# Attention with a local window and a low-rank mixer MLP on one core: q and k turned by VectorE, off-diagonal keys in a tile of their own, a written order

## The chip, the cores and the metric

The kernel runs on one NeuronCore of a Trainium2 chip. The metric is the device time of one execution in microseconds (us). One execution was also profiled; times below that have two decimals come from it and count from the start of its span. Engines: TensorE (PE; PEld is its weight load), VectorE (DVE), ScalarE (ACT), GpSimd (POOL), SyncE (SP, whose instructions here are DMA issues only). DMAs are issued by POOL (queue q0) and by SP (queue q1) and carried by 16 DMA engines.

## The reference

Four batches, 8 heads, 768 tokens, head size 64. Attention keeps the first 8 keys and, for each query, the 96 last ones, with a bias that falls with distance; its output, rows of 512, goes through a mixer over tokens of rank 32 and a two-layer MLP of 2048.

```python
# q, k, v: (4, 8, 768, 64)   n_global = 8, n_local = 96
scores = scale * np.matmul(q, k.transpose(0, 1, 3, 2))
rel = pos[:, None] - pos[None, :]
is_global = pos[None, :] < n_global
is_local = (rel >= 0) & (rel < n_local)
dist = np.where(is_global & ~is_local, n_local, np.abs(rel))
scores = np.where(is_global | is_local, scores - slopes * dist, -1e9)
a = softmax(scores)
x = (a @ v) with the heads side by side                # (4, 768, 512)
h = x.transpose(0, 2, 1) @ U @ V                       # U: (768, 32), V: (32, 768)
u = x + h.transpose(0, 2, 1)
out = u + np.maximum(u @ w_ch1, 0.0) @ w_ch2           # 512 -> 2048 -> 512, float32
```

## The kernel before

All products are float16 with float32 sums. A *pair* is two heads of one batch; there are 16, p = 0 to 15, four for each batch. The work is cut into named tasks, each a handful of instructions on one engine. Names carry the pair, or the batch and a number:

- `lk`, `lq`, `lv` (`ld`, line 450, and `ldv`, line 460) load k, q, v of a pair on POOL's queue, cast from float32 to float16 on the way. Pair 0's k and q come by SP in float32 and are cast by `Ck0`, `Cq0`. Of the first seven pairs but that one, q comes with 6 tokens to a partition (one run of 1536 bytes for each partition and head) and k with three groups of 2 tokens (runs of 512 bytes). Pairs 7 to 15 come in runs of 256 bytes (one token of one head), 1,536 for each q, k or v, in two issues for q and k and in one for v.
- `TK`, `TQ` (line 600) turn k and q so that the head's columns are the partitions: 12 TensorE transposes each, for pairs 0 to 6, and `EK`, `EQ` copy the result out of PSUM. For pairs 7 to 15 `EK`, `EQ` are DMA transposes on SP (line 624).
- `KO` (line 643) puts the 32 first keys beside each block of keys. A block of queries meets its own block of keys (the diagonal) and one off-diagonal block: the last 96 keys of the block before, and the first 32. In this kernel those lie side by side because each block of `kT` is 160 wide. `VO` and `VG` (lines 650 to 660) build the rows of v that belong to it, which shifts them by 32 partitions: in pairs 0 and 1 by POOL copies, from pair 2 on by a DMA on SP.
- `SB` adds the bias of batch 0 into PSUM as a product of the identity with a table for each head (line 689); `S` are the scores (line 708), row-tiled, so that two heads of 64 rows share the array; `EX` the exp on ACT; `MK` multiplies by exp of the bias (masks) on DVE in batches 1 to 3.
- `PV` is the product with v (lines 804, 805), `RC` and `NM` divide by the sums, `XC` casts x to float16, `UP` (lines 778, 788) turns x by six products with the identity and forms x times U by six products with u as weights; `TE` copies the latter out, `HM` (line 911) adds the product with V, `E0` to `E1` copy u into `uT`. For pairs 12 to 15 x is turned by a DMA transpose on SP (`XD`, line 880) and added by DVE.
- `M1a`, `M1b` (line 967) are the first MLP product, 16 steps a batch, `RL` their relu on ACT. The second is done by seven half-size products instead of eight: `PA`, `PB` and `TW` make the sums and differences on DVE, `RS` (line 1035) brings in the mixer, `P1` to `P7` (line 1047) are the products for three token blocks, `DI`, `DA` to `DH` add them up, `O` stores a row block.

Which task stands where is set by a planner: it plays the tasks on the five engines with estimated durations and picks, on each engine, the ready task with the lowest priority number. `PRIO` overrides these numbers for some tasks. The instructions are then written out in the order of the planned starts, so each engine runs its tasks in a fixed order. Before the first `M1a`, gaps that the planner sees on TensorE are filled with products of zeros (line 1118).

```python
ready.append((max(r, clock[e]), t.prio, t))
...
first = min(r[0] for r in ready)
s, _, t = min((r for r in ready if r[0] <= first + self.hold[e]), key=lambda r: (r[1], r[0]))
```

Buffers: three stages each for q and k, four for v, three for the turned q and k. PSUM has eight banks; attention of batches 1 to 3 uses four of them and the MLP four. The attention of batch b+1 stands between the products of batch b's MLP.

Of the kernel before, what the change touches and what calls it, by code (L numbers as in the profile page):

```python
# [11 lines left out]
FP16 = mybir.dt.float16  # L12
# [4 lines left out]
PE, ACT, DVE, POOL, SP = "PE", "ACT", "DVE", "POOL", "SP"  # L17


PRIO = {  # L20
    "DA0.1": 9974.7, "DA1.1": 2084.0, "DA1.2": 1446.2, "DA2.1": 7573.6, "DA2.2": 168.5, "DB0.0": 381.3,
    "DB0.1": 824.4, "DB0.2": 1435.8, "DB1.0": 648.9, "DB1.1": 9380.8, "DB1.2": -715.0, "DB2.0": 1750.3,
    "DB2.1": 7394.5, "DB2.2": 921.0, "DB3.0": 4247.8, "DB3.1": 1752.8, "DC0.0": 1445.9, "DC0.1": 241.1,
    "DC0.2": 3950.9, "DC1.2": -1125.0, "DC3.0": 4597.3, "DD0.0": -369.8, "DD0.1": 1451.6, "DD0.2": 7547.4,
    "DD1.0": 5644.0, "DD1.2": 1790.9, "DD2.2": 1857.9, "DD3.0": 9079.6, "DE0.0": 4526.5, "DE0.1": 4818.3,
    "DE0.2": 1899.6, "DE1.0": 1079.9, "DE1.1": 1235.7, "DE1.2": 9688.2, "DE2.0": 9329.5, "DE2.1": 7182.2,
    "DE3.1": 408.9, "DF0.0": -587.1, "DF0.1": 906.3, "DF0.2": 1308.3, "DF1.0": 1987.4, "DF1.1": 4335.1,
    "DF1.2": 9220.2, "DF2.1": 1119.2, "DG0.0": 1566.3, "DG0.1": 1561.2, "DG0.2": 4753.1, "DG1.1": 1049.2,
    "DG2.0": 1258.8, "DG3.0": 8393.9, "DH0.1": -943.2, "DH0.2": 7144.0, "DH1.0": 4329.3, "DH1.2": 1416.7,
    "DH2.0": 1090.1, "DH2.2": 9290.0, "E01": 680.8, "E012": 6952.3, "E015": 6662.8, "E02": 1709.4,  # L30
    "E03": 7455.6, "E115": 6744.6, "EK1": 1092.1, "EK11": 1175.1, "EK2": -4286.2, "EK3": 1889.8,
    "EQ0": 5977.3, "EQ1": 1795.7, "EQ2": 3871.2, "EQ3": 1123.3, "EQ4": 2337.6, "EQ5": -70.1,
    "EX0.0": 136.1, "EX0.1": 619.4, "EX0.2": 1542.8, "EX1.0": -44.8, "EX1.2": 651.6, "EX10.0": -3388.7,
    "EX10.1": -4484.6, "EX11.0": 671.9, "EX12.0": 259.7, "EX12.1": 848.5, "EX13.1": 2805.7, "EX14.0": -4053.9,
    "EX15.0": 325.5, "EX15.1": 1245.1, "EX2.2": 459.5, "EX3.2": -4609.0, "EX4.0": 2040.9, "EX4.1": 708.4,
    "EX5.1": -3545.6, "EX5.2": 2671.0, "EX6.0": 277.4, "EX7.1": 1490.6, "EX8.0": 484.1, "EX8.1": 473.6,
    "EX9.0": -4173.8, "EX9.1": 528.5, "HM1": 7237.6, "HM10": 1056.5, "HM11": 2789.4, "HM12": 193.4,
    "HM13": 4578.0, "HM14": 2924.3, "HM4": 1390.4, "HM6": 6847.2, "HM7": 7112.0, "HM8": 875.8,
    "KO1": 4413.7, "KO10": 4820.4, "KO13": 1045.3, "KO4": 1558.1, "KO6": 7458.7, "KO8": 810.0,
    "KO9": 5696.5, "MK10.1": -64.6, "MK10.2": 8941.2, "MK11.0": 1790.4, "MK11.1": 6926.2, "MK11.2": 4176.4,  # L40
    "MK12.1": 9457.0, "MK12.2": 9396.4, "MK14.0": 1575.4, "MK15.0": 2089.4, "MK5.0": 1157.0, "MK5.1": 4456.1,
    "MK5.2": 4026.8, "MK6.1": 1969.0, "MK6.2": 8473.4, "MK7.0": 1965.2, "MK7.2": 8877.9, "MK8.0": 4742.7,
    "MK8.2": 7363.9, "NH3.0": 1052.5, "NH3.1": 4293.2, "NH3.2": -718.0, "NM0": 3502.3, "NM10": -3.6,
    "NM12": 745.7, "NM13": 4324.7, "NM2": 956.8, "NM3": 8933.0, "NM4": 6531.1, "NM6": 9302.7,
    "NM8": 8671.5, "NM9": 5709.1, "P10.0": 8038.9, "P10.1": 3749.7, "P10.2": 1100.2, "P11.0": 7486.8,
    "P11.1": 779.5, "P11.2": 890.3, "P12.0": 258.9, "P12.1": 1917.5, "P12.2": -195.3, "P13.0": 1231.1,
    "P13.1": 5474.6, "P13.2": 1092.0, "P20.0": 6169.2, "P20.1": 6444.0, "P20.2": 1493.3, "P21.0": 81.1,
    "P21.1": 196.4, "P21.2": 6738.9, "P22.0": 7741.1, "P22.1": 7201.7, "P22.2": 4091.2, "P23.0": -41.9,
    "P23.1": 1721.9, "P23.2": 7210.2, "P30.0": 7173.3, "P30.1": 6570.0, "P30.2": 1800.3, "P31.0": 7984.8,
    "P31.1": 4608.1, "P31.2": 1074.6, "P32.0": 284.8, "P32.1": 7089.9, "P32.2": 738.2, "P33.0": 8514.1,  # L50
    "P33.2": 9035.8, "P40.0": 8007.7, "P40.1": 3973.5, "P40.2": 6133.8, "P41.0": 3854.4, "P41.1": 7361.7,
    "P41.2": 6492.4, "P42.1": 7111.9, "P42.2": 1850.0, "P43.0": 5388.4, "P43.1": -217.2, "P43.2": 8297.9,
    "P50.0": 7151.2, "P50.1": 7171.5, "P50.2": 1808.9, "P51.0": 6511.1, "P51.1": 3837.9, "P51.2": 806.0,
    "P52.0": 2789.2, "P52.1": 7444.2, "P52.2": 988.2, "P53.0": 3222.2, "P53.1": 8488.0, "P53.2": 5964.3,
    "P60.0": 1544.3, "P60.1": 7428.3, "P60.2": 6759.4, "P61.0": 3319.6, "P61.1": 3970.3, "P61.2": 5190.3,
    "P62.0": 6224.9, "P62.1": 7152.4, "P62.2": 804.9, "P63.0": 4221.3, "P63.1": 480.6, "P63.2": 802.1,
    "P70.0": 6565.8, "P70.1": 8670.9, "P70.2": 4740.0, "P71.0": 6930.4, "P71.1": 3484.2, "P71.2": 2866.8,
    "P72.0": 5944.4, "P72.1": 7444.2, "P72.2": 7101.8, "P73.0": 5747.6, "P73.1": 6207.0, "P73.2": 4226.5,
    "PA0.1": 3875.7, "PA1.1": 4773.6, "PA2.3": 4018.7, "PB0.0": 4368.4, "PB0.1": 3979.1, "PB1.0": 4691.2,
    "PB1.1": 4947.3, "PB1.2": 581.7, "PB1.3": 5664.9, "PB2.1": 9613.8, "PB2.2": 6977.8, "PB2.3": 1205.4,  # L60
    "PV1": 953.8, "PV10": 6764.8, "PV11": 1576.6, "PV12": 7016.6, "PV13": 4620.5, "PV14": 4609.9,
    "PV2": 4453.8, "PV3.1": 7591.7, "PV3.2": 6559.2, "PV4": 3559.8, "PV5": 5520.0, "PV6": 6732.0,
    "PV8": 8381.2, "PV9": 6620.1, "RC1": 1068.7, "RC10": -348.8, "RC3.0": 85.5, "RC3.1": 1705.7,
    "RC3.2": 1515.9, "RC4": 1577.1, "RC5": 572.7, "RC6": 9411.2, "RC9": 4947.8, "RS0.0": 623.7,
    "RS0.1": 7972.9, "RS0.2": -1247.9, "RS1.0": 667.2, "RS1.1": 4419.1, "RS1.2": 657.7, "RS2.0": 6902.5,
    "RS2.1": 3723.0, "RS2.2": 7418.7, "RS3.0": 200.0, "RS3.1": -174.3, "RS3.2": 8.1, "S0.0": 1224.9,
    "S0.1": 1257.7, "S0.2": 597.8, "S1.1": 6958.1, "S1.2": 408.5, "S10.2": 925.1, "S11.0": 2116.4,
    "S11.2": 2864.1, "S12.0": 7724.4, "S12.2": 1228.1, "S13.0": 2772.6, "S13.2": 6865.5, "S14.0": 1199.9,
    "S14.2": 2407.7, "S15.0": 1398.4, "S15.2": 4794.4, "S2.0": 7510.6, "S2.2": 4999.8, "S3.0": 1728.1,
    "S3.2": 3575.4, "S4.0": 7303.6, "S4.2": 7813.1, "S5.0": 7633.1, "S5.2": 6453.5, "S6.0": 1492.8,  # L70
    "S6.2": 2826.3, "S7.0": 2695.5, "S7.2": 5594.9, "S8.0": 6717.1, "S8.2": 6990.7, "S9.0": 3459.0,
# [44 lines left out]
class Planner:  # L116
# [19 lines left out]
    def pick(self, g, taken=()):  # L136
        free = self.free[g.kind]
        best = None
        for i in g.among if g.among is not None else range(0, len(free) - g.n + 1, g.n):
            if (g.kind, i) in taken:  # L140
                continue
            f = max(free[i:i + g.n])
            if f < 1e8 and (best is None or f < best[0]):
                best = (f, i)
# [1023 lines left out]
```

## Time and profile before

| | |
|---|---|
| time, median of 3 runs | 234.32 us (233.78 to 234.71) |
| the profiled execution, span from first to last instruction | 231.3 us |
| granted TensorE clock | 1.00 in every slice |
| busy: PE, PEld, DVE, ACT, POOL | 97%, 68%, 66%, 51%, 39% |
| queue q0 (POOL), packets and bytes written | 63,616, 13.24 MB |
| queue q1 (SP), packets and bytes written | 26,000, 13.35 MB |
| HBM read, written | 27.46 MB, 6.29 MB |

The two columns of a busy group are its engine's time and the mean duration of one instruction; the idle time after the second bar is the engine's just before these instructions. A matmul's duration is its time through the array, so matmuls overlap, and what one costs is read from the chain or from the distance of starts. "DMA share" counts the packets under way over 16 engines and can be above 1.

### The profile page before, as it was taken

How to read it: one execution, taken by the hardware profiler on the slowest of the kernel's cores; microseconds unless marked ns; L12 is line 12 of the kernel's file. 1: busy time of each engine (PE TensorE's matmuls, PEld its weight loads, DVE VectorE, ACT ScalarE, POOL GpSimd, SP SyncE). 2: the span in 40 equal slices, each digit the busy share in tenths (PEclk: the TensorE clock that was granted, in tenths of full speed). 3: DMA queues.
4: the chain of work that ended last, by engine and by line, in shares of the span. 5: the costliest groups of instructions: out<-in, count | busy, mean ns of one | idle time of the engine just before them, and what ended most of it. 6: DMA issues, size and time to landing. Idle time of an engine off the chain costs nothing.

```text
span 231.3 us, 5732 instructions
## 1 busy us (share of the span) xinstructions
PE 223.4 (97%) x2402; PEld 158.3 (68%) x2402; DVE 153.1 (66%) x321; ACT 118.7 (51%) x161; POOL 90.2 (39%) x116
## 2 busy tenths in 40 slices
PE   7889999999999999999999999999999999999993
PEld 2556675565788885656678885666689875658882
DVE  6548772499987975375867785395888840626762
ACT  3576978878632446766652228868610025662000
POOL 9789968349929960264800911030100000000000
PEclk9999999999999999999999999999999999999999
DMA  7999999999999999992961995221020630000025
GB/s 169 162 163 150 156 189 211 207 188 166 167 157 160 175 166 235 219 123 22 130 56 41 162 162 173 56 41 30 15 22 17 157 136 4 0 0 3 0 84 191
DMA packets 89642, 26.96 MB, mean 117 GB/s; under 512 B 77040, under 2 KB 86640, under 8 KB 89616
## 3 DMA queue, kind: packets, MB, share of 16 engines
q0 software_dynamic: 63616, 13.24, 69.3%
q1 hardware_dynamic: 26000, 13.35, 27.3%
q8 instruction: 19, 0.31, 0.5%
q14 instruction: 7, 0.06, 0.1%
HBM read 27.46 MB, written 6.29 MB: 146 GB/s over the span
## 4 chain that ended last, share of the span: by engine, by line
PE 84%; POOL 7%; DMA 6%; issue 1%; ACT 0%; DVE 0%; POOLq 0%
PE ps L967 37%; PE ps L1047 33%; PE ps L708 4%; DMA vt<-in_v_dram 3%; DMA stgk<-in_k_dram 3%; PE ps L805 2%; PE ps L788 2%; POOL vo L368 2%; PE ps L804 2%; PE ps L1035 1%; POOL stgk L453 1%; POOL vt L461 1%; PE ps L778 1%; PE ps L911 1%; POOL stgq L453 1%
## 5 line engine op out<-in xcount | busy, mean ns | idle before, releaser
L967 PE MATMUL ps<-uT,w 128*128 128x384 f16 x512 | 88.1, 326 | 0.3 <-ACT uT L364 0.3
L967 PEld LDWEIGHTS <-w 128*128 128x128 f16 x512 | 48.1, 98 | 32.2 <-issue 1.0
L984 ACT ACTIVATE htr<-ps 128x768 f16<-128x768 f32 x64 | 51.9, 811 | 32.4 <-PE ps L967 32.2
L735 ACT ACTIVATE ep<-ps 128x1024 f16<-128x1024 f32 (+1 forms) x48 | 44.1, 952 | 16.0 <-PE ps L708 15.9
L1047 PEld LDWEIGHTS <-htr 128*128 128x128 f16 x384 | 36.1, 98 | 6.5 <-issue 2.0
L1047 PEld LDWEIGHTS <-sA 128*128 128x128 f16 x288 | 27.5, 98 | 3.8 <-issue 0.5
L461 POOL DMA_DIRECT2D vt<-in_v_dram x16 | 16.5, 1031 | 34.4 <-PE ps L805 27.9
L748 DVE TENSOR_TENSOR ep<-ep,mask 128x1024 f16<-128x1024 f16 x24 | 16.6, 691 | 16.4 <-ACT ep L735 16.4
L1060 DVE TENSOR_TENSOR x_sb<-ps,x_sb 128x256 f32<-128x256 f32 x48 | 19.9, 421 | 9.9 <-PE ps L1047 9.4
L1047 PE MATMUL ps<-w,htr 128*128 128x256 f16 x192 | 24.5, 273 | 0.0
L1047 PE MATMUL ps<-tB,htr 128*128 128x256 f16 x192 | 24.4, 273 | 0.0
L1047 PE MATMUL ps<-w,sA 128*128 128x256 f16 x192 | 24.4, 273 | 0.0
L368 POOL COPY vo<-vt 32x650 f16<-32x650 f16 x22 | 18.1, 823 | 9.5 <-DMA vt<-in_v_dram 8.9
L1001 DVE TENSOR_TENSOR sA<-htr 128x768 f16<-128x768 f16 x16 | 9.5, 594 | 18.3 <-ACT htr L984 18.1
L364 ACT ACTIVATE u<-ps 128x256 f32<-128x256 f32 x12 | 4.6, 384 | 29.7 <-PE ps L1047 29.7
L869 POOL CAST x<-x_sb 128x768 f16<-128x768 f32 x12 | 10.8, 906 | 22.7 <-DVE x_sb L843 12.8
L457 POOL DMA_DIRECT2D stgk<-in_k_dram x18 | 14.8, 834 | 3.8 <-PE ps L967 3.8
L708 PEld LDWEIGHTS <-kT 64*128 64x128 f16 x352 | 10.1, 94 | 8.9 <-issue 8.1
L457 POOL DMA_DIRECT2D stgq<-in_q_dram x18 | 14.9, 838 | 3.1 <-DMA w<-in_moe_w_ch_dram 3.1
L708 PE MATMUL ps<-qT,kT 64*128 64x128 f16 x352 | 15.6, 218 | 0.0
L843 DVE TENSOR_TENSOR x_sb<-ps,rcp 128x768 f32<-128x768 f32 x16 | 15.2, 956 | 0.4
L1060 DVE TENSOR_TENSOR u<-ps,u 128x256 f32<-128x256 f32 x24 | 10.0, 419 | 6.7 <-PE ps L1047 4.9
(78 smaller groups left out, 272.2 us busy)
## 6 DMA issues: line engine op xcount, KB each, us to landing
out_dram<-x_sb SPq DMA_DIRECT2D x23, 256.0 KB, 2.6
w<-in_moe_w_ch_dram POOLq DMA_DIRECT2D x8, 512.0 KB, 9.2
vt<-in_v_dram POOLq DMA_DIRECT2D x16, 192.0 KB, 7.1
stgk<-in_k_dram POOLq DMA_DIRECT2D x18, 96.0 KB, 6.8
stgq<-in_q_dram POOLq DMA_DIRECT2D x18, 96.0 KB, 6.2
vo<-vt SPq DMA_DIRECT2D x14, 121.9 KB, 4.9
stgk<-in_k_dram POOLq DMA_DIRECT2D x6, 192.0 KB, 6.7
stgq<-in_q_dram POOLq DMA_DIRECT2D x6, 192.0 KB, 6.6
```

What stands on the lines that cost most here:

```text
L368: nc.gpsimd.tensor_copy(dst, src)
L457: nc.gpsimd.dma_start(o[:, :, hi], src[b, h0 + hi].rearrange("(n p) d -> p n d", p=P))
L461: nc.gpsimd.dma_start(vt[gv.slot][:, :, :, 0:D], v[b, h0:h0 + 2].rearrange("h (n p) d -> p h n d", p=P),)
L708: nc.tensor.matmul(t[:, hi, j * P:(j + 1) * P], lhs, qt[r, i * P:(i + 1) * P], start=not biased, stop=True, skip_group_check=biased,)
L735: nc.scalar.activation(ep[gep.slot][:, :, lo:512], ps[:, gsc.slot:gsc.slot + 2, lo:512], AF.Exp, scale=qk_scale)
L748: nc.vector.tensor_tensor(ev, ev, mv, ALU.mult)
L843: nc.vector.tensor_tensor(xo, pvo()[:, :, :, 0:D], rcp[p % 2].unsqueeze(3).broadcast_to((P, 2, NB, D)), ALU.mult)
L869: (nc.vector if xe == DVE else nc.gpsimd).tensor_copy(x16[gx16.slot], src)
L967: nc.tensor.matmul(ps[:, g.slot + half, 0:HS], w1[:, dc, jt * P:(jt + 1) * P], ub[:, dc, half * HS:(half + 1) * HS], start=(dc == 0), stop ...
L984: nc.scalar.activation(htr[:, jt].rearrange("p (h c) -> p h c", h=2), ps[:, g.slot:g.slot + 2, 0:HS], AF.Relu)
L1047: nc.tensor.matmul(o, a[:, j, c0 + cols.start:c0 + cols.stop], bq[:, j], start=False, stop=(j == hj - 1), skip_group_check=True,)
L1060: return lambda: e.tensor_tensor(o(), x(), y(), ALU.add)
```

## The change

In words:

- Loads: in batch 0 k is read like q, 6 tokens to a partition. For pairs 4 to 15 q and k are read so that one partition holds 32 columns (one half j of a head) of 24 tokens in a row: runs of 32 float32 (128 bytes), 1,536 in each of two issues, each writing 64 partitions.
- Turning: pairs 4 to 15 use one DVE instruction for each q and k, `nc.vector.transpose`, which turns blocks of 32 by 32 and writes them with a stride of 24 elements. The TensorE transposes and PSUM copies of pairs 4 to 6 and the 18 DMA transposes of pairs 7 to 15 are gone.
- Off-diagonal keys: a new tile `kO` holds them in place, the last 96 of the block before and the first 32 over the first rows, where the v tile `vo` now holds its rows without a shift. `KO` is two copies on POOL, ACT, DVE or SP; `VO` becomes `VC` (a copy of whole blocks) and `VG` (the first 32 rows), each on an engine chosen for each pair.
- Bias of batch 0: the weights are the identity times the head's slope (`ib`) and the moving table `rel3` is shared, instead of eight tables.
- Low-rank products: for pairs 4 to 15 x is the stationary side, with 32 columns of u moving; `XE` copies the sum out and `XU` turns it with the identity. The DMA transposes of x for pairs 12 to 15 are gone; they use TensorE like the others.
- Engines of single tasks (casts, copies, evictions) are set for each pair by letters, and some `HM` are full-height instead of row-tiled.
- Order: `PRIO` is gone, and one list of all tasks, `ORDER`, is walked in its order; the planner keeps the buffers and the fill-in products. `lk1` is the first POOL task. Batch 0's q and k are issued before its v. `S4.0` stands before the first `M1a`, six of the eight masks after it.

```diff
-PRIO = {
-    "DA0.1": 9974.7, "DA1.1": 2084.0, "DA1.2": 1446.2, "DA2.1": 7573.6, "DA2.2": 168.5, "DB0.0": 381.3,
...
+ORDER = """
+vz lk1 wz iota relf bias3 rel3 bias7 TK1 EK1 bias2 SB1.0 SB1.1 KO1 bias0 lk0 Ck0 lq1 ones0 TQ1 EQ1 TK0 EK0 back
+bias4 bias6 lq3 S1.0 EX1.0 bias5 S1.1 lk3 TK3 EK3 lq2 SB1.2 S1.2 TQ2 lq0 Cq0 TQ3 EX1.1 EQ3 KO3 TQ0 EQ0 lk2 TK2 bias1
...
+NH3.1 UP3.1 NH3.2 UP3.2 TE3 HM3 E03 E13 NM3 S4.0 EX4.0 EX4.1 MK4.1 lq5 TD0 M1a0.1 w1_2 M1b0.1 RL0.1 M1a0.0 M1b0.0
...
+""".split()
+CFG = {
+    "TK": "PPPPDDDDDDDDDDDD", "TQ": "PPPPDDDDDDDDDDDD", "NU": (4, 5, 6, 7, 8, 9, 10, 11, 12, 13, 14, 15),
...
+    "HR": "RFFRRRRRRRRRFRFR", "RR": "RRRRRRRRRRRR", "IB": "DADDDDDD", "U16": "D", "VS": "APDP", "C0": "DD",
+    "VO": "PDDPDPPPDDSSSSSA", "XC": "PDPDPPPAPAAPPDDP", "E": "AAAAAAAAAAAAAAAA",
 }
-CFG = {'petr': (4, 5, 6), 'E': 'DAD', 'VO': 'PPSSSSSSSSSSSSSS', 'ML': (2,), 'XT': (12, 13, 14, 15), 'HMT': True}
...
-    kT = sb("kT", [P, NB, PK], FP16, N_QK)
+    kT = sb("kT", [P, NB, P], FP16, N_QK)
+    kO = sb("kO", [P, NB - 1, P], FP16, N_QK)
...
-                    o = dst[g.slot].rearrange("p a b -> p (a b)").rearrange("p (n h d) -> p n h d", n=NB, h=2)
-                    for hi in range(2):
-                        nc.gpsimd.dma_start(o[:, :, hi], src[b, h0 + hi].rearrange("(n p) d -> p n d", p=P))
+                    o = dst[g.slot].rearrange("p a b -> p (a b)")
+                    for i in range(2):
+                        nc.gpsimd.dma_start(
+                            o[64 * i:64 * i + 64], src[b, h0 + i].rearrange("(t k) (j e) -> j t k e", t=TB, j=2)
+                        )
...
+        def turn(dst, stg, gs):
+            def go():
+                nc.vector.transpose(
+                    dst().rearrange("c (t k) -> c k t", t=TB),
+                    stg[gs.slot].rearrange("p a b -> p (a b)").rearrange("p (k e) -> p k e", e=TB),
+                )
...
-            kt = kT[gkT.slot]
-            copy(ke, kt[:, 0:NB - 1, P:PK], kt[:, 0:1, 0:32].broadcast_to((P, NB - 1, 32)))
+            kt, ko = kT[gkT.slot], kO[gkT.slot]
+            copy(ke, ko[:, :, GP:P], kt[:, 0:NB - 1, GP:P])
+            copy(ke, ko[:, :, 0:GP], kt[:, 0:1, 0:GP].broadcast_to((P, NB - 1, GP)))
...
-                    bb = bias[:, h0 + hi]
-                    if s:
-                        bb = bb[:, 128:384].unsqueeze(1).broadcast_to((P, 2, 256))
-                    nc.tensor.matmul(t[:, hi, lo:512], ident16, bb, start=True, stop=False, skip_group_check=True)
+                    bb = rel3[:, 128:384].unsqueeze(1).broadcast_to((P, 2, 256)) if s else rel3
+                    nc.tensor.matmul(t[:, hi, lo:512], ib[:, h0 + hi], bb, start=True, stop=False, skip_group_check=True)
...
-                        lhs = kt[r, i - 1, 32:PK] if j % 2 == 0 else kt[r, i, 0:P]
+                        lhs = ko[r, i - 1] if j % 2 == 0 else kt[r, i]
```

The products of the low-rank step, whose code was there but not used by any pair before (`xu` is now true for pairs 4 to 15):

```python
if xu:
    nc.tensor.matmul(ps[:, gx.slot, 384:384 + R], xx[:, c], u16[:, c, 0], start=False, stop=(c == NB - 1))
...
copy(ENG[CFG["XE"][p]], xus[gxu.slot], ps[:, gx.slot, 384:384 + R].unsqueeze(1).broadcast_to((P, RG, R)))
nc.tensor.matmul(ps[:, gx.slot + 1, 384:512], xus[gxu.slot].rearrange("p g r -> p (g r)"), ident16, start=False, stop=True)
```

## The prediction

> **What bounds the kernel now.** I read four views. The first is the chain of waits in order of time.
>
> ```profile
> 25.42 0.99 POOL vt L461
> 26.41 6.84 DMA stgk<-in_k_dram
> 33.25 0.04 issue
> 33.29 0.53 PE ps L600 x12
> ...
> 35.16 2.71 PE ps L967 x16
> ...
> 208.99 18.46 PE ps L1047 x168
> 227.47 0.42 DVE x_sb L1060
> ```
>
> Columns: start, duration, what. From 33.3 us to 227.5 every piece but 0.9 us at 87.6 (an ACT eviction) is TensorE. Before 33.3 the chain runs through POOL and a key load. So there are two levers: how early the first product (L967) starts, and how much TensorE work follows. The timeline of TensorE has the first product's start:
>
> ```profile
> 35.09 2.12 PE L967 MATMUL ps<-uT,w 128*128 128x384 f16 x12
> ```
>
> The busy times by stretch tell what else is near its limit (stretch, length, PE, PEld, DVE, ACT, POOL, clock, DMA share, GB/s):
>
> ```profile
> 0.00:35.09 35.09, 31.38 (x482) 20.10 (x483) 23.55 (x58) 24.20 (x38) 29.61 (x46) 1.00 1.34 165
> 35.09:60.20 25.11, 25.11 (x228) 15.16 (x226) 17.17 (x29) 19.27 (x25) 16.85 (x20) 1.00 1.67 189
> 60.20:88.50 28.30, 27.99 (x360) 22.60 (x360) 23.65 (x54) 12.51 (x17) 20.48 (x25) 1.00 2.05 170
> ```
>
> Before 35 us TensorE's 31.4 us include fill-in products, so nothing is full there: the stage is a chain of waits. From 60 to 88 DVE is busy for 84% and the DMA engines overlap two packets each (share 2.05). The groups and the queues give the prices:
>
> ```profile
> L600 PE MATMUL ps<-ident,stgk 128*64 128x128 f16 x84 | 4.0, 236 | 1.8 <-DMA stgk<-in_k_dram 1.7
> L366 DVE COPY qT<-ps 128x768 f16<-128x768 f16 x4 | 3.8, 956 | 1.8 <-PE ps L600 1.8
> L461 POOL DMA_DIRECT2D vt<-in_v_dram x16 | 16.5, 1031 | 34.4 <-PE ps L805 27.9 <-issue 5.2 <-DMA w<-in_moe_w_ch_dram 1.0
> L457 POOL DMA_DIRECT2D stgk<-in_k_dram x18 | 14.8, 834 | 3.8 <-PE ps L967 3.8
> ```
> ```profile
> q0 software_dynamic: 63616, 13.24, 69.3%
> ...
> out_dram<-x_sb SPq DMA_DIRECT2D x23, 256.0 KB, 2.6
> ...
> out_dram<-x_sb SPq DMA_DIRECT2D x2, 128.0 KB, 1.9
> kT<-stgk SPq DMA_TRANSPOSE x9, 6.1
> ```
>
> **The change, part by part.**
>
> *TensorE after the first product.* Pair 6's transposes go: two groups of 12, each 0.46 us in the chain (34.70 to 35.16 is one), -0.9. S4.0 (0.50 in the chain) moves ahead of the first product, -0.5. Row-tiled visits cost a change of mode: 8 score products take 0.33 and 14 take 0.50, so 0.028 each and 0.11 for going in and out. Counted along both orders, changes of mode after the first product fall from 74 to 60: 14 x 0.053 = -0.7. Two mixing steps (pairs 12 and 14) become full-height: 2 x 0.16 = +0.3. The low-rank products of pairs 4 to 11 keep six identity products (0.33 for six) and trade six of 128 columns (0.34) for six of 32 columns plus one turn of 0.056. A 32-column product is not in this trace; the nearest row is the 65-column one, 0.031 us, its floor is nothing. At 0.031 a pair saves 0.34-0.19-0.06 = 0.09, eight pairs 0.8. Pairs 12 to 15 lose their DMA-turned x and gain 0.33+0.19+0.06-0.34 = 0.24 each, +1.0. Net +0.2 (at zero cost -2.0); I take +0.2. Sum: **-1.6** (-3.8 to -1.6).
>
> *The start.* ACT had 22.9 us of work (24.2 less the 1.3 table load) between 4.06 and 35.09, so 8.1 us of gaps, 5.9 of them ended by a transpose of L600, most of these by late q or k. In the new order ACT has ahead of the first M1b: two k evictions of one 768-column copy each (0.81, as ACT's qT copies), KO1 0.75, twelve exps (4 x 0.81 + 8 x 1.02 = 11.4), EQ3 0.81, bias1 0.2, two masks 1.0, vs0 0.46, two TE 0.6, E01, E00, E02 2.4, one exp of pair 4 1.0, E13 0.5: 20.8. It begins at about 6.5: lk1 is issued first (0.8 us earlier than now) and k now comes in 1536-byte runs, 256 packets instead of 768. With no gaps the first product starts at 27.3, with all of today's gaps at 35.4. All q and k of batch 0 now go out before any v, and late q and k ended most of the gaps, so I take some 60% of them off, 30.5: **-4.6** (-7.8 to +0.3). It must also find w1_0 landed. Ahead of w1_0 on the queue are 6 q/k, 4 v, lk4 and lq4; at the 60-to-88 rate, 16 x 2.05 / 40.3 ns (69.3% of 16 x 231.3 us over 63,616 packets) = 814 packets per us, up to 1,140 in the busiest stretch of the packet records. v is 1.5 us, a pair's turned q or k (3,072 packets) 2.7 to 3.8, a weight quarter 0.52 MB at 200 GB/s = 2.6, a token-wise one 1.0. From 3.5 us: 6 + 6 + 5.4 + 2.6 makes 23.5, and with the copies of POOL in between 26: in time.
>
> *Edits at nothing.* The eight bias tables (0.34 each on DVE) become eight third-width ones; DVE has 11 us free in that stage. Six of eight masks (0.52 each on ACT) go behind the first relus, where ACT is busy 19.3 of 25.1 us; without that room each would hold a relu, and its bank pair, 0.5.
>
> *The turned q and k.* 24 loads of 2 issues with 1,536 runs each: POOL pays L461's 1.03 per issue, 48 x 1.03 = 49 us against 36 x 0.83 + 6 x 0.8 (pairs 4 to 6) = 35 now. POOL is 39% busy and has 7 us or more of slack per batch: nothing on the path. The queue grows from 63,616 packets to about 104,000, at 814 per us 78 to 128 us of 231. But by 41 us it must have brought lk5, lq5, w1_2 and w1_3 too: 26 + 1.5 (lv4) + 2.6 + 2 x 2.7 to 3.8 + 2.6 = 38 to 40 for w1_2, which is asked for at 30.5 + 5 x 1.31 + 1 = 38. The wait is 0 to 4 us; I take **+1.2**.
>
> *DVE.* A turn has no row here. The nearest is the 768-column copy, 0.956; below it the f32-to-f16 cast of stgq, 0.56; above it twice the copy, if 48-byte write strides cost. I take 0.92. In batch 0's product stage DVE had 23.65 of 28.3; six turns (5.5) come, KO6 to KO8 (3 x 0.3) and XC7 (0.8) go: 27.5 of 28. DVE's queue is in order, so behind a turn whose load is late stand DC, DA and DB, which free the banks that P6, P7 and P4 need. I take **+1.5** (0 to +5). Batches 1 and 2 have 34 of 50 and 35 of 48 busy now; eleven and five turns fit.
>
> *The 18 + 4 DMA transposes, new KO, VC and VG copies.* SP loses 22 issues of about 1.2 us and 6.1 us of flight; what they hid behind was two pairs of lead, so nothing is gained; if the copies that replace them (KO on POOL, about 0.95) come late, a score step waits about 1 us. Zero.
>
> *The tail.* The last store is now half a row (128 KB, 1.9) instead of a whole one (2.6): **-0.5** of 0.7.
>
> Sum: -1.6 - 4.6 + 1.2 + 1.5 - 0.5 = **-4.0**. The profiled execution spans 231.3; the median 234.3 is 3.0 above it (start and end outside the span, and the run). 231.3 - 4.0 + 3.0 = **230.3**.
>
> **The rivals.**
>
> *Two engines for a turned load (slower).* The new source pattern's outermost step has a count of 2 (the two halves j of a head's columns), where every load now has 128. If a transfer is split over the engines by that count, each carries 768 packets in order on one engine: 768 / (814/16) = 15 us instead of 3. lk4 and lq4 (issued at 13 to 17) land at 29 to 32, and EK4 heads DVE's queue ahead of NM2, UP3 and E03: first product at 34.5 instead of 30.5. w1_2 and w1_3 queue behind lk5 and lq5 (landing 43): wait 2.5 instead of 1.2. EK6 waits some 2 us more than it does now. -4.0 + 4.0 + 1.3 + 2 = +3.3: **237.6**. It decides from a landing time of about 9 us on. For it: nothing in the loads of now has such a pattern, so nothing speaks against it; against it: the destination still has 64 partitions, which could be split instead. The Trainium skill (DMA: Bandwidth & Descriptors, section on why a DMA increments its semaphore by 16) states just this: the slowest dimension of both sides sets how many engines a DMA uses, the largest number up to 16 that divides both, which would be 2 here, though it notes that some direct copies from the GpSimd queue use 16 all the same. No run here shows it; by that rule the time would be this rival's.
>
> *The start does not move.* ACT's gaps come back elsewhere (35.1): the rest, -1.6 + 1.5 - 0.5, no w1 wait: 231.3 - 0.6 + 3.0 = **233.7**. For it: 23 us of DVE work stand in the same stage. Against: its queue had 11 us free there.
>
> *DVE becomes the bound.* A turn of 1.5 us: 6 x 0.6 = 3.5 more in batch 0's products, little elsewhere: **233.8**. For it: 84% busy now; against: DVE's other 768-column rows are all 0.56 to 0.96.
>
> **How the numbers follow.** Forecast 0.62, two engines 0.16, start 0.12, DVE 0.10. Forecast's own range 226.5 to 233: the bounds of start and waits half-way. The range reaches into the others: 226 to 237. A measurement tells 0.5% (1.2 us) from no change. Faster: nearly all of the forecast and a third of the two middle rivals, 0.68; same: the rest of these, 0.14; slower 0.18.
>
> **What would show it.** The first product of w1 and uT at 28 to 32 us (35 refutes the main term). Landing of the turned k and q below 9 us; 15 or more is the two-engine rival. TensorE's gaps between 36 and 46 us released by w, and from 55 to 85 by DVE. The turn's mean near 0.92 us. The 32-column products at 0.03 us. If TensorE stands still after 90 us for 2 us or more, the forecast has missed something.

## The result: 945.61 us, four times as long, with the profile after

The changed kernel took 945.61 us (median of 4 runs, 944.68 to 949.55) against 234.05 us for the kernel before, measured beside it: a ratio of 4.05 [4.03, 4.07]. The forecast was 230.3. The profiled execution spans 942.9 us. Its first MLP product (now line 839) starts at 93.42 us instead of 35.09, and behind it TensorE stands still again and again; its granted clock averages 0.63, against 1.00 before. The page, top to bottom: the packets of POOL's queue, the shares of the chain by engine, the turned loads, the turn, and the time from issue to landing of a v and a turned load.

```profile
q0 software_dynamic: 621280, 15.31, 50.6%
...
issue 60%; POOL 22%; PE 11%; DMA 4%; DVE 2%; ACT 0%; POOLq 0%; DVEq 0%
...
L385 POOL DMA_DIRECT2D stgq<-in_q_dram x24 | 100.7, 4197 | 287.5 <-issue 287.5
L385 POOL DMA_DIRECT2D stgk<-in_k_dram x24 | 100.8, 4200 | 264.0 <-issue 262.7
...
L506 DVE STREAM_TRANSPOSE qT<-stgq 128x768 f16<-128x768 f16 x12 | 44.1, 3710 | 232.9 <-DMA stgq<-in_q_dram 232.9
...
vt<-in_v_dram POOLq DMA_DIRECT2D x16, 192.0 KB, 12.2
stgk<-in_k_dram POOLq DMA_DIRECT2D x24, 96.0 KB, 16.6
```

Three things stand out. A turned load's issue occupies POOL for 4.2 us, where a load of as many runs (v, 1.03) was a quarter of that. It lands after 16.6 us. And POOL, ahead of the 48 issues, waits some 550 us in all for something that the trace calls "issue", that is, for no other instruction. The queue has 621,280 packets, where 104,000 were expected. The chain of waits, in order of time (start, duration, what), shows the rhythm:

```profile
18.01 4.22 POOL stgk L385
22.24 12.31 issue
34.56 4.20 POOL stgk L385
38.77 12.43 issue
```

A transfer takes 16.6 us in the median (16.2 to 18.5), and the next issue starts when the last has landed, not before: the first lands 16.2 us after its issue at 18.01, and the second is issued at 34.56. 48 times 16.7 is 802 us; the first of them is issued at 18.0 us and the last at 827.0. Before, the chain from 33 us on was TensorE; now that engine has 11% of it.

In the packet records of the after run, 517,344 of the queue's packets have 4 bytes. That is exactly 48 x (14 x 768 + 16) + 30 x 16: each turned transfer puts 768 runs of data on each of two engines, and on each of the other fourteen 768 packets of 4 bytes that carry no data; the 16 more, which the queue's other 30 transfers have too, are one for each engine at its end.

### The profile page after: what moved, and what is told of

It reads as the page before. It is cut to its first block, busy times and chain, and to the rows that moved or that the text cites. A ratio compares the mean times of both kernels' runs of the same rounds, so it can differ in the third digit from the quotient of the medians.

```text
span 942.9 us, 5595 instructions
## 1 busy us (share of the span) xinstructions
PE 249.4 (26%) x2338; PEld 171.8 (18%) x2338; DVE 234.0 (25%) x328; ACT 130.1 (14%) x190; POOL 254.3 (27%) x123
## 2 busy tenths in 40 slices
DMA packets 630713, 24.16 MB, mean 26 GB/s; under 512 B 620032, under 2 KB 627712, under 8 KB 630688
## 3 DMA queue, kind: packets, MB, share of 16 engines
q0 software_dynamic: 621280, 15.31, 50.6%
## 4 chain that ended last, share of the span: by engine, by line
issue 60%; POOL 22%; PE 11%; DMA 4%; DVE 2%; ACT 0%; POOLq 0%; DVEq 0%
POOL stgk L385 10%; POOL stgq L385 9%; PE ps L918 4%; PE ps L839 4%; DMA stgk<-in_k_dram 2%; DMA stgq<-in_q_dram 2%; DVE qT L506 1%; POOL vt L391 1%; DVE kT L506 1%; PE ps L607 1%; POOL vo L301 1%; POOL x L764 1%; PE ps L588 0%; PE ps L491 0%; POOL kO L301 0%
## 5 line engine op out<-in xcount | busy, mean ns | idle before, releaser
L385 POOL DMA_DIRECT2D stgq<-in_q_dram x24 | 100.7, 4197 | 287.5 <-issue 287.5
L385 POOL DMA_DIRECT2D stgk<-in_k_dram x24 | 100.8, 4200 | 264.0 <-issue 262.7
L506 DVE STREAM_TRANSPOSE qT<-stgq 128x768 f16<-128x768 f16 x12 | 44.1, 3710 | 232.9 <-DMA stgq<-in_q_dram 232.9
L506 DVE STREAM_TRANSPOSE kT<-stgk 128x768 f16<-128x768 f16 x12 | 44.8, 3730 | 196.1 <-DMA stgk<-in_k_dram 196.1
L675 PE MATMUL ps<-ident,x 128*128 128x128 f16 x96 | 12.1, 243 | 255.3 <-POOL x L764 164.3
L607 PE MATMUL ps<-qT,kO 64*128 64x128 f16 x160 | 15.6, 251 | 204.8 <-POOL kO L301 134.9
L701 PE MATMUL ps<-vo,ep 128*128 128x65 f16 x160 | 14.4, 210 | 206.7 <-POOL vo L301 182.9
L675 PEld LDWEIGHTS <-x 128*128 128x128 f16 x96 | 9.5, 118 | 257.0 <-POOL x L764 165.4
L702 PEld LDWEIGHTS <-ep 128*128 128x128 f16 x192 | 15.3, 108 | 208.7 <-issue 207.8
L607 PEld LDWEIGHTS <-kO 64*128 64x128 f16 x160 | 8.9, 108 | 210.7 <-POOL kO L301 155.9
L918 PEld LDWEIGHTS <-htr 128*128 128x128 f16 x384 | 39.2, 107 | 25.6 <-issue 18.5
## 6 DMA issues: line engine op xcount, KB each, us to landing
stgk<-in_k_dram POOLq DMA_DIRECT2D x24, 96.0 KB, 16.6
stgq<-in_q_dram POOLq DMA_DIRECT2D x24, 96.0 KB, 16.6
```

The lines of the kernel that those rows point to most:

```text
L385: nc.gpsimd.dma_start(o[64 * i:64 * i + 64], src[b, h0 + i].rearrange("(t k) (j e) -> j t k e", t=TB, j=2))
L506: nc.vector.transpose(dst().rearrange("c (t k) -> c k t", t=TB), stg[gs.slot].rearrange("p a b -> p (a b)").rearrange("p (k e) -> p k e", ...
L607: nc.tensor.matmul(t[:, hi, j * P:(j + 1) * P], lhs, qt[r, i * P:(i + 1) * P], start=not biased, stop=True, skip_group_check=biased,)
L675: nc.tensor.matmul(ps[:, gx.slot + c // 3, (c % 3) * P:(c % 3 + 1) * P], xx[:, c], ident16, start=(c % 3 == 0), stop=False, skip_group_che ...
L701: nc.tensor.matmul(o, e[:, hi, j * P:(j + 1) * P], vof[:, hi, i - 1, 0:D1], start=True, stop=False)
L702: nc.tensor.matmul(o, e[:, hi, (j + 1) * P:(j + 2) * P], vv[:, hi, i, 0:D1], start=(i == 0), stop=True)
```

## The experiments

Ratios are to the kernel before, measured beside each run; runs 1 to 3 are one execution each. The recorded expectations call some runs by a label: e2 is run 5, e4 run 4, e7 run 6, e9 run 8, e10 run 9 and e11 run 11.

**1. The outermost step of two taken away.** Each transfer is split by its half j; run lengths, bytes and the turn are the same.

```diff
-                        nc.gpsimd.dma_start(
-                            o[64 * i:64 * i + 64], src[b, h0 + i].rearrange("(t k) (j e) -> j t k e", t=TB, j=2)
-                        )
+                        for j in range(2):
+                            nc.gpsimd.dma_start(
+                                o[64 * i + 32 * j:64 * i + 32 * j + 32],
+                                src[b, h0 + i].rearrange("(t k) (j e) -> j t k e", t=TB, j=2)[j],
+                            )
```

> The changed kernel, but each turned load goes out as four transfers of 768 runs, one for each head and half j, so that no access pattern has an outermost count of 2 (32 partitions on one side, 768 runs on the other). Runs, packets and layout in SBUF are the same. Theory (the outermost count of 2 puts a transfer on two engines, and POOL's next issue waits until it has drained): landings fall from 16.6 us below 9, the half million 4-byte packets are gone, POOL's 4.2 us issues fall to about 0.6 each, and the time falls to 250 to 300 us, which the 3.7 us turns on DVE then set (234 us of DVE work in the profile). Rival (64-byte packets from 128-byte runs are slow in themselves): landings stay above 12 us, time above 700 us.

Measured: 296.54 us, 649 less. The page of this run, with the queue, the load and the turn:

```profile
q0 software_dynamic: 105952, 13.25, 71.5%
...
L508 DVE STREAM_TRANSPOSE kT<-stgk 128x768 f16<-128x768 f16 x12 | 44.7, 3722 | 0.0
...
L386 POOL DMA_DIRECT2D stgk<-in_k_dram x48 | 34.0, 715 | 3.2 <-DMA w<-in_moe_w_ch_dram 2.5
...
stgk<-in_k_dram POOLq DMA_DIRECT2D x48, 48.0 KB, 3.3
```

The packets without data are gone, a load lands in 3.3 us, an issue takes 0.72. The turn still takes 3.7 us and DVE has 31% of the chain: it is a second, smaller fault of the change.

**2. As many transfers, but with the step of two.** This tells the pattern from the count and the size of the transfers: 16 of the 32 token groups, both halves.

```diff
+                        for g_ in range(2):
+                            nc.gpsimd.dma_start(
+                                o[64 * i + 32 * g_:64 * i + 32 * g_ + 32],
+                                src[b, h0 + i, 384 * g_:384 * g_ + 384].rearrange("(t k) (j e) -> j t k e", t=16, j=2),
+                            )
```

> The twin of the kernel with the halves apart: also four transfers of 768 runs for each load, to 32 partitions each, but each holds both halves j of 16 token groups, so its source again has an outermost count of 2. The rows of a stage stand in another order, so q and k are permuted in this run. Theory (outermost count): two engines again, 384 runs on each, 4-byte packets as many as before, 96 transfers of about 8.3 us, so 800 to 950 us in all; if POOL waits only because a second transfer of 768 runs on an engine does not fit beside the first, the waits shrink and the time is 500 to 800. Rival (short runs as such): the same time as the kernel with the halves apart.

Measured: 694.73 us, and 622,048 packets on the queue again. 518,112 of these have 4 bytes, which is 96 x (14 x 384 + 16) + 30 x 16: two engines with 384 runs each carry a transfer. In run 1 only 2,016 have 4 bytes, 16 for each of 126 transfers. Same bytes, same number of transfers, same run length and partitions as in 1: the step of two is the cause. The timeline of POOL in this run (start, duration, what, idle time before):

```profile
16.04 4.82 POOL L386 DMA_DIRECT2D stgk<-in_k_dram  x2
26.39 2.35 POOL L386 DMA_DIRECT2D stgk<-in_k_dram  x1 [5.53 <-issue]
31.28 2.35 POOL L386 DMA_DIRECT2D stgk<-in_k_dram  x1 [2.53 <-issue]
```

Two transfers of 384 entries for each engine go out back to back; the third starts 10.35 us after the first, which has landed by then (10.0 us from issue to landing). With 768 entries each, as in the changed kernel, not even the second goes out beside the first. My reading is that the queue holds a limited number of entries for each engine, and that the empty ones fill the fourteen idle engines' share of it as well; the runs show the rhythm, not the queue's size itself.

**3. The new load alone in the kernel before** (pairs 7 to 15; its products use numbers in the wrong places, since the DMA transposes behind are those of the old layout).

```diff
-                    o = dst[g.slot].rearrange("p a b -> p (a b)").rearrange("p (n h d) -> p n h d", n=NB, h=2)
+                    o = dst[g.slot].rearrange("p a b -> p (a b)")
                     for hi in range(2):
-                        nc.gpsimd.dma_start(o[:, :, hi], src[b, h0 + hi].rearrange("(n p) d -> p n d", p=P))
+                        nc.gpsimd.dma_start(
+                            o[64 * hi:64 * hi + 64], src[b, h0 + hi].rearrange("(t k) (j e) -> j t k e", t=32, j=2)
+                        )
```

> The kernel before with one part of the change: q and k of pairs 7 to 15 are read by the new pattern; its order, its DMA transposes and everything else stay (the transposes then turn data that lie otherwise, so q and k of these pairs are not the reference's). Theory (the load alone does it): 36 transfers of 16.7 us, about 600 us of POOL's time in place of 30, so 650 to 780 us. Rival (the new order or the turns on DVE hold the transfers up): 232 to 245 us.

Measured: 756.12 us, as the theory had it. The load's group has the same price as in the changed kernel, in a kernel that has nothing else of the change:

```profile
L457 POOL DMA_DIRECT2D stgq<-in_q_dram x18 | 75.5, 4194 | 224.0 <-issue 224.0
```

**4. The change without its loads and turns**: 256-byte runs and DMA transposes in pairs 4 to 15, as the kernel before has them from pair 7 on.

```diff
-            if p not in by_pe and turned[x][p] == "D":
-                return add(DVE, 0.92, turn(dst, stg, gs), [ld], acq=[gt], rel=[gs], name=f"E{x}{p}")
+            if p not in by_pe:
...
+                return add(SP, 1.3, dtr, [ld], acq=[gt], rel=[gs], size=2.8, name=f"E{x}{p}")
```

> The changed kernel with one part undone: q and k of pairs 4 to 15 come in 256-byte runs (two transfers of 768) and are turned by DMA transposes on SP, as pairs 7 to 15 in the kernel before; new order, keys in place, low-rank products, bias and engines stay as changed. Theory (load and turn alone cost the time): 226 to 238 us, first MLP product at 28 to 32 us as forecast. Rival (the new order is itself bad): above 245 us.

Measured: 247.56 us, ratio 1.0586 [1.0494, 1.0679]. The number is the rival's, but the place speaks against it: two waits of TensorE for late turns, 7.0 and 5.1 us, are most of the 14.3 us lost. The second is for a copy `kO` that itself waited 16.6 us for its turned k, as the last line says.

```profile
PE ps L611 <- POOL kO L301: 7.0, 3, 5.1
PE ps L611 <- DMA qT<-stgq: 7.0, 1, 7.0
POOL kO L301 <- DMA kT<-stgk: 36.0, 4, 16.6
```

The order was written for a turn of 1 us; a DMA transpose here takes 4.3 us (k) and 4.8 us (q) from issue to landing in the median and up to 10.7. So this run doesn't tell what the order is worth behind the start. The start it does tell: the first product came at 34.37 us, not at 28 to 32, although no load of this run goes to two engines.

**5. A turn that writes densely.** On top of 1, tokens are dealt as k x 32 + t instead of t x 24 + k: the loads are as before in number and length, but a turned block is now written as 32 neighbours and not with a stride of 24 elements.

```diff
-                    dst().rearrange("c (t k) -> c k t", t=TB),
+                    dst().rearrange("c (k t) -> c k t", t=TB),
```

> The kernel with the halves apart, and the tokens dealt to the partitions the other way round (token k*32+t in place of t*24+k), so that the turn on DVE writes each block of 32 columns side by side and not with a stride of 48 bytes. Theory (the stride of the writes costs the turn its 3.7 us): a turn takes 0.8 to 1.2 us, DVE's work falls from 229 to about 170 us, time 228 to 245 us. Rival (blocks of 32 by 32 cost 3.7 us for 768 columns however they are written): the turn stays at 3.7 us and the time at about 297 us.

Measured: 239.39 us, ratio 1.0248 [1.0204, 1.0291]. All turns of k in this run (min, median, max in ns):

```profile
L508 DVE STREAM_TRANSPOSE kT<-stgk x12: 923/968/978, 26.3 to 148.0; 128x768 f16<-128x768 f16 x12
```

0.97 against 3.7 us: the write stride had cost 2.75 us for each of 24 turns, 66 us of DVE, and 57 us of time. What is left over the kernel before points to POOL. The largest waits of TensorE name its copies of v (total, times, longest):

```profile
PE ps L703 <- POOL vo L301: 5.8, 3, 2.7
```

and the windows show the stretch (length, then busy time and count of PE, PEld, DVE, ACT, POOL, then clock, DMA share, GB/s):

```profile
60.00:88.00 28.00, 24.10 (x296) 19.36 (x297) 23.70 (x39) 13.63 (x24) 27.94 (x38) 0.94 1.56 69
```

POOL is busy for 27.94 of 28 us, 19 of them with issues of turned loads: 0.71 us each, four for a q or k.

**6. POOL's copies moved away.** The v copies of pairs 0, 3, 5, 6, 7 to SP as DMAs, KO to ACT, three casts to ACT. A string has one letter for each pair: P for POOL, D for DVE, A for ACT, S for SP.

```diff
-"KO": "PADDDPAAAPPPAPPS"
+"KO": "PADDDAAAAAAAAAAS"
-"VO": "PDDPDPPPDDSSSSSA", "XC": "PDPDPPPAPAAPPDDP"
+"VO": "SDDSDSSSDDSSSSSA", "XC": "PDPDAAAAPAAPPDDP"
```

> The kernel with halves apart and the dense turn (e2, 239.39 us), with copies taken off POOL: in pairs 0, 3, 5, 6 and 7 the v copies (VC, VG) become DMAs on SP, KO of pairs 5 and 9 to 14 goes to ACT (also from DVE's letter P), x casts (XC) of pairs 4, 5 and 6 go to ACT. Theory: what is left of the loss in e2 is POOL's queue: its 96 load issues (68.4 us) keep POOL busy 27.9 of the 28 us from 60 to 88, and three PV steps wait 2.1, 1.4 and 2.85 us behind its v copies, and w1_0 is issued 3.3 us late at 25.8. With some 8 + 5 + 3 us of copies gone those waits fall away: 232 to 236 us, PE gaps released by vo under 1 us each, w1_0 issued before 23.5 us, first product below 33.5. Rival: the queue's transfers (runs of 128 bytes, 106,000 packets, 88% share) hold it, so POOL's copies only hide a wait for data: 238 to 240 us, with the gaps now released by DMA stgk, stgq, vt or w. Second rival: ACT, 54% busy, and its queue pay for the moved work: PE gaps released by ACT, 238 or more.

Measured: 242.33 us, ratio 1.0385 [1.0325, 1.0445]: a miss. The first product went from 34.8 to 39.1 us, since the DMA copies of v in pairs 0 and 3 came later than POOL's, and only the time behind it fell, from 202.8 to 200.4.

**7. Halves apart and a dense turn in the kernel before** (pairs 7 to 15, instead of DMA transposes).

```diff
-            EK = add(SP, 1.3, base + 1, dtr(kT, gkT, stgk, gk), [tk], acq=[gkT], rel=[gk], size=2.8, name=f"EK{p}")
+            EK = add(DVE, 0.8, base + 1, dvt(kT, gkT, stgk, gk), [tk], acq=[gkT], rel=[gk], name=f"EK{p}")
```

> The kernel before, with its own tasks and planner, where only q and k of pairs 7 to 15 change: loaded with halves apart (4 issues, 32 partitions each, token k*32+t) and turned by one dense VectorE turn instead of a DMA transpose. Theory: the turn itself is no gain on the path, since the DMA transposes were hidden, and POOL pays 18 x (4 x 0.713 - 2 x 0.834) = 21 us more for issues and DVE 18 x 0.97 = 17 us: POOL 39% to some 48%, DVE 66% to 73%, both below full outside a stage or two: 233 to 238 us (first product unchanged at 35, no PE gap above 3 us). Rival: taking 18 DMA transposes (6.1 us each, 13 MB of queue 1) off the DMA engines speeds the loads: below 232 us. Rival: runs of 128 bytes are too slow for the loads even over 16 engines (each load lands after 4 us or more and PE waits for it): above 240.

Measured: 272.86 us, ratio 1.1672 [1.1609, 1.1735]; loads landed in 3.2 (q) and 3.6 us (k) in the median, below the bound of the second rival. No expectation held. The old kernel's planner lays the whole order out anew when a task moves to another engine, and its new order has scores waiting for DVE (7.7 us, five times) and gaps of up to 4.0 us from 150 to 184 us; the granted clock is 0.50 from 160 to 186 us, and the first six 384-column products behind the gaps follow each other by 0.32 us instead of 0.16. The run prices an order, not the turn, and is inconclusive.

**8. As 6, with the v copies of pair 0 on DVE and of pair 3 on ACT.**

```diff
-"VO": "SDDSDSSSDDSSSSSA"
+"VO": "DDDADSSSDDSSSSSA"
```

> As the run with POOL relieved (e7, 242.33 us, span 239.5), but the v copies of pair 0 go to DVE and of pair 3 to ACT and not by DMAs on SP; pairs 5, 6 and 7 stay with SP. In e7 the first product of the MLP stood at 39.1 us (34.8 in e2) and 200.4 us followed it (202.8 in e2, 196.2 in the kernel before). Theory: POOL's copies in front of 88 us were worth the 2.4 us that e7 gained after the first product, and e7's late start came from the DMA copies of v in pairs 0 and 3 alone: first product 32.5 to 35 us, 200 to 201 us after it, span 233 to 236, 235 to 238 us in all. Rival: the start is held by the 24 issues of turned loads and w1 on POOL's queue (lk4, lq4, lk5, lq5 before the first product) and by ACT, so the first product is at 36 or later whatever engine copies v: 238 to 242.

Measured: 237.60 us, ratio 1.0147 [1.0086, 1.0208]; first product at 34.80 us, 200.9 us after it. As the theory had it. But TensorE now waits for the copies where they were put:

```profile
PE ps L609 <- ACT kO L295: 3.3, 3, 1.6
...
PE ps L677 <- ACT x L764: 1.6, 3, 0.7
PE ps L703 <- DMA vo<-vt: 1.5, 2, 1.2
```

**9. Loads that cost next to nothing**, to price the rest of the change: one transfer of 128 long runs for each q and k.

```diff
+                        if i == 0:
+                            nc.gpsimd.dma_start(o, src[b, h0:h0 + 2].rearrange("h (t k) e -> (h t) (k e)", t=64))
```

> The changed kernel with a dense turn, where q and k of pairs 4 to 15 come in one transfer of 128 runs of 3072 bytes instead of 2 with 1,536 runs of 128 bytes: the same bytes, but each row of 12 tokens stays where it lies and is not dealt to the halves, so the scores of pairs 4 to 15 are those of other numbers; all instructions behind the loads are the same. Theory: the loads (issues on POOL and packets on the queue) are all that stands between the rest of the change and a time near the forecast: POOL has 24 x 0.8 = 19 us of load issues instead of 68 and the queue some 17,000 packets: 228 to 232 us, PE behind the first product 195 to 198 us. Rival: the new order, engines and low-rank products give nothing by themselves (e4, the new order with DMA transposes, had 247.6): 233.7 or more, first product at 34 or later and PE gaps that no load ends.

Measured: 226.68 us, ratio 0.971 [0.9652, 0.9767]; 34,144 packets on the queue; the first product starts at 31.06 us:

```profile
31.06 6.66 PE L838 MATMUL ps<-uT,w 128*128 128x384 f16 x40 [0.25 <-DVE uT L297]
```

Its window of 60 to 88 us stands against that of run 5:

```profile
60.00:88.00 28.00, 27.71 (x332) 20.66 (x331) 25.57 (x50) 17.16 (x28) 12.66 (x18) 1.00 0.74 111
```

POOL 12.66 instead of 27.94 us, TensorE 27.71 instead of 24.10. Against run 5, the 128-byte runs with their issues cost 12.7 us (239.39 less 226.68). The 7 us against the kernel before are the worth of the order, the engines, the dense turn and the low-rank products together with loads that are cheaper than those of the kernel before too (34,144 packets against 63,616); no run takes these apart. In both figures, 1.5 to 2 us may be the chance of run 9's early start (see the last section).

**10. TensorE at full speed sooner.** In the new order the zero tile for the fill-in products is written behind the first load; here DVE writes it first, and three more fill-ins stand ahead of the first real product. Else as 5.

```diff
-    c_wz = add(POOL, 0.5, lambda: nc.gpsimd.memset(zero16, 0.0), name="wz")
+    c_wz = add(DVE, 0.3, lambda: nc.vector.memset(zero16, 0.0), name="wz")
...
-vz lk1 wz iota relf
+wz vz lk1 iota relf
...
-                    idle(int(gap / 0.43), 512, bank)
+                    idle(int(gap / 0.43) + 3, 512, bank)
```

> Halves apart and dense turn (e2, 239.39 us) with the zero tile written first, by VectorE (in the new order POOL writes it behind the first load, so TensorE's fill-in products start at 2.66 us instead of 1.32), and three more fill-in products of 512 columns before the first real one. In e2, e9 and the changed kernel TensorE still runs at half speed (105 ns for two 128-column transposes, 53 at full speed) until past 10 us; in the kernel before it is at full speed from 7.3 us, in the run with long rows (e10) from 6.6. Theory: some 1.5 to 2 us of the late first product (34.8) is this: full speed from 7.5 us or sooner, first product at 32.5 to 33.5, 237 to 238.2 us. Rival: the first 10 us are hidden behind POOL's issues and v copies, which are as before: first product 34.3 or later, 239 or more.

Measured: 241.01 us, ratio 1.0331 [1.0261, 1.0401], not below run 5, although the first product came at 32.63 us, 2.15 sooner and within the theory's range. TensorE waited for POOL's copies, 2.7 us until 80.4 and 2.4 us until 99.9, as in run 5 (2.7 and 2.3 us): it looks as if POOL's queue sets the end of that stretch whenever the stretch begins. The start was right and the total wrong.

**11. The start of 10, and most of the copies of 8 on DVE** (the diff against 10).

```diff
-"KO": "PADDDPAAAPPPAPPS"
+"KO": "PADDDDAAADDDADDS"
-"VO": "PDDPDPPPDDSSSSSA", "XC": "PDPDPPPAPAAPPDDP"
+"VO": "DDDADDSSDDSSSSSA", "XC": "PDPDDPDAPAAPPDDP"
```

> The same, and POOL's copies moved once more: KO of pairs 5, 9, 10, 11, 13 and 14 to DVE right behind the turn (e9 had them on ACT, and PE waited 3.3 us for them), the v copies of pairs 0 and 5 on DVE, of 3 on ACT, of 6 and 7 by SP, the x casts of pairs 4 and 6 on DVE (pair 5 as in e9 or before on POOL or DVE). Theory: e9's waits after the first product (9.0 us in eight gaps, all but one behind moved copies) fall to 3 to 5 and the start comes 1.5 to 2 us sooner: span 227 to 231, 229.5 to 233 us, so better than the kernel before. Rival: DVE, 68% busy in e9 and 84% from 60 to 88 in the kernel before, becomes the bound from 60 to 110, with PE gaps ended by DVE: 234 to 237 us. Second rival: the 96 issues of loads alone keep q and k late: gaps ended by DMA stgk or stgq, 235 to 238.

Measured: 233.99 us, ratio 1.0028 [0.9994, 1.0063], level with the kernel before and between the theory and its rival. The first product came at 34.15 us. DVE did not become the bound; two waits for v copies on it, 1.7 us until 22.2 and 2.0 us until 65.1, are the largest gaps once TensorE works. The second copy, pair 5's, stands on DVE behind the turns of pair 6's k and q. The timeline of POOL shows why pair 6 is late: six transfers of weights are issued just ahead of its loads (35.97 to 42.58), and five of the eight issues of q and k start when one of them has landed. Three of these:

```profile
47.56 0.71 POOL L386 DMA_DIRECT2D stgq<-in_q_dram  x1 [1.50 <-DMA w<-in_moe_w_ch_dram]
50.21 0.71 POOL L386 DMA_DIRECT2D stgk<-in_k_dram  x1 [1.95 <-DMA w<-in_moe_w_ch_dram]
52.75 0.71 POOL L386 DMA_DIRECT2D stgk<-in_k_dram  x1 [1.83 <-DMA w<-in_moe_w_ch_dram]
```

**12. The v copies sooner in DVE's queue** (the diff against 11).

```diff
-"VO": "DDDADDSSDDSSSSSA"
+"VO": "DDDDDDSSDDSSSSSA"
-lq4 VC2 u16 VG2 VC0 SB2.1 S2.1 VG0 EX0.1
+lq4 VC0 VG0 VC2 u16 VG2 SB2.1 S2.1 EX0.1
-PB0.1 EK6 DC0.0 EQ6 lv6 VC5 lk7 VG5 PV5
+PB0.1 VC5 VG5 EK6 DC0.0 EQ6 lv6 lk7 PV5
```

> As the run that is level with the kernel before (e11, 233.99 us, ratio 1.0028), with v copies sooner in DVE's queue: those of pair 0 ahead of those of pair 2, those of pair 3 on DVE and not on ACT, and those of pair 5 ahead of the turn of pair 6's k (EK6), whose load is late because POOL's issues stand in the full queue from 43 to 57 us. In e11 PE waited 1.9 us (20.3) and 2.2 us (62.9) for them. Theory: these two waits are what is left over the kernel before: the first product from 34.15 to 32.5 or 33, the gap at 62.9 under 0.7: span 228 to 230, 230 to 232.5 us, ratio 0.985 to 0.995. Rival: the loads of pair 6 and 7 are late themselves, so the wait moves from the v copies to the scores of pair 6 (PE gaps ended by the turned kT or qT at 64 to 72) and the start waits for ACT: 233 to 235, ratio 0.995 to 1.006.

Measured: 232.52 us, ratio 0.9935 [0.9906, 0.9963]; first product at 31.69 us, the wait for pair 5's v copies down to 0.5 us. The time is at the top of the theory's range, the start sooner than it said. This version is faster than both kernels, by 0.65% against the one before: little, but outside the interval. It has all of the change but the load's pattern, the turn's stride, the late zero tile and the engines and places of some copies. The largest gap left in its profile (of the longest of its nine executions), 2.6 us until 80.9, waits for a v copy made by a DMA on SP.

## Why the prediction was wrong, point by point

*The turned load: the step that failed.* The forecast let a pair's q or k land after 2.7 to 3.8 us, at 814 packets per us over all engines, and took the pattern's outermost count of 2 into a rival with a chance of 0.16. A transfer took 16.6 us. Runs 1 and 2 show that it is this count (296.5 without it, 694.7 with it at the same number of transfers), and run 3 that the new load alone makes 756 us of the kernel before. The Trainium skill (DMA: Bandwidth & Descriptors, section on why a DMA increments its semaphore by 16) has the rule, and the trace agrees: 768 runs on each of two engines. The exception for some copies from GpSimd's queue, also noted there, did not apply. It is not the only step: with the loads landing in 3.3 us and the turn at 0.97, as forecast, run 5 still takes 239.39 us, beyond the forecast's 226 to 237. The rest is in the terms below.

*The rival's price.* Its landing time was right: 15 us against 16.6. Its total, 237.6, was wrong by 708 us, because it charged the delay of the few loads that the path meets first and let the rest overlap. 48 x 15 was never multiplied out. POOL waited before each issue until the transfer ahead had landed, so the transfers are a strict sequence: 802 us.

*POOL.* The forecast gave 49 us for the issues and "nothing on the path". It was 201 us in the changed kernel. Even with the halves apart it is 68.4 (96 x 0.71), and that fills POOL from 60 to 88 us: the second step that failed. With the packets of the short runs it makes the 12.7 us between runs 5 and 9; which of the two costs more was not told apart. The forecast's own case, 48 issues of 1,536 short runs spread over 16 engines, is in no run.

*The turn.* 0.92 was taken, with 1.9 as the upper bound if strides cost. With the stride it is 3.7 us, twice the bound; dense it is 0.97. So the price fitted the instruction and not the pattern it wrote. Its cost was 57 us (run 1 to run 5); in the changed kernel the loads cover it, since DVE idles 232.9 us ahead of the turns of q, waiting for them.

*The start.* -4.6 to 30.5 was forecast. With the changed order the first product came at 34.37 us in run 4, 34.78 in run 5 and 34.80 in run 8, hardly sooner than the 35.09 before: a third step that failed, and what these runs show is the rival of a start that does not move (35.1). One thing was left out of the sum. The order that brings lk1 forward puts the zero tile behind it, so TensorE's fill-in products begin at 2.67 us instead of 1.32, and in these three runs its first products run at half speed until 10.0 to 11.7 us. With the fill-ins sooner, the first product came at 32.63 in run 10, with POOL's issues as in run 5, at 34.15 in run 11 and at 31.69 in run 12; in run 9, at full speed from about 6 us and with cheap loads, at 31.06. So the gain is there to be had, but for the most part by an edit that the change lacks. The wait for w1 in run 5 was 1.2 us, as forecast.

*TensorE and DVE after the first product.* Run 9 needs 193.1 us (224.2 less 31.06) where the kernel before needed 196.2: -3.1, where the terms -1.6, -0.5, +1.2 and +1.5 sum to +0.6. The stalls did not come: no wait of TensorE behind the start is above 0.3 us there, and DVE runs 25.57 of 28 us without holding it. The product behind a 32-column one starts 0.026 us after it (0.031 was taken), so the TensorE terms are a little larger than -1.6, within their bounds. Run 9's 226.7 us lies at the lower end of the forecast's range, but that is partly luck: its loads (24 issues, 34,144 packets) are cheaper than those forecast (48 issues, some 104,000 packets).

## What to carry to other kernels

Before a load's run length, look at the outermost step of both its sides: where it was 2 here, two engines carried everything. Price a stream on one queue by the sum of its transfers and of its issues on the engine that makes them, not by the delay of the first. And a transposing instruction has the price of the pattern that it writes: choose how the tokens are dealt in the load so that its output is dense.

## What the runs showed of the hardware that was not expected

*Idle engines are not idle in the queue.* 14 x 768 packets of 4 bytes for each two-engine transfer, 82% of all packets (517,344 of 630,713).

*A DVE copy can last as long as an issue on POOL.* In the changed kernel, while POOL issued the first turned load (18.01 to 22.23), two small copies on DVE took 3.92 us, against 0.42 in run 1:

```profile
18.53 3.92 DVE L297 COPY kO<-kT 128x480 f16<-128x480 f16 x2
```

The Trainium skill (SBUF — State Buffer, section Who interferes with whom) says that a copy on VectorE that uses two ports shares a pair of ports with GpSimd and waits for a whole instruction there; the trace agrees. It is no single case: all five copies from SBUF to SBUF on DVE that met such an issue (at 18.5, 88.4, 122.8, 502.6 and 538.6 us, 1.2 to 3.8 us long) ended 0.11 to 0.13 us after the issue did, while two casts out of PSUM beside issues took 0.3 us each and the turns kept their 3.7 us.

*TensorE's first products ran at half speed for a time that differs.* The same four bias products in the timeline of run 5 (start, duration):

```profile
8.38 1.70 PE L590 MATMUL ps<-rel,ib 128*128 128x384 f16 x4
```

and in that of run 9:

```profile
7.44 0.92 PE L587 MATMUL ps<-rel,ib 128*128 128x384 f16 x4
```

The profile prints a granted clock of 1.00 for both stretches, but the first clock record in the trace (full speed) is at 10.04 us in run 5 and at 6.10 in run 9; the print has nothing to go by ahead of it. In both runs the fill-ins began at 2.67 us and the instructions ahead are the same. Of the eight profiles with fill-ins that late, seven reach full speed 7.4 to 9.2 us after the first fill-in and run 9 alone after 3.4, so some 1.5 to 2 us of run 9's early start may be chance; run 10 got there by starting the fill-ins sooner. The Trainium skill (TensorE: Matmul & The Clock Gate, Part 1) states that the array starts at half rate, rises after about 3.4 us of work and that this differs from run to run, since the window that is watched runs freely. The two executions agree in that it differs; the 3.4 us fit run 9, and not the 7.4 of run 5, where TensorE stood still for 1.36 us in between (1.11 in run 9).
